# A retention layer with soft mixture of experts on one core: cleared tiles, a maximum kept as a column, eight PSUM banks for the last products, and inputs split into rows of 6 KB and 2 KB

## The chip, the cores and the metric

The kernel runs on one core of a Trainium2 chip. The metric is the device time of one execution in microseconds (us), as a median of several runs. The core's engines are called PE (TensorE, matrix products), DVE (VectorE), ACT (ScalarE), POOL (GpSimd) and SP (SyncE, which here issues all DMAs). All data is float32.

## What is computed

The inputs q, k and v have the shape (4 batches, 8 heads, 768 tokens, 64). A retention layer runs over the tokens, and its output, with the heads side by side (3072 tokens, 512 columns), goes through a soft mixture of 8 experts with 4 slots each:

```python
# retention, gamma[h] = 1 - 2**(-5-h)
for t in range(S):
    state = gamma * state + outer(k[:, :, t], v[:, :, t])
    y[:, :, t] = q[:, :, t] @ state / sqrt(D)
# soft mixture of experts, x = y as (3072, 512)
logits = x @ phi                                # (3072, 32 slots)
d = softmax(logits, over tokens)
slot_input = d.T @ x                            # (32, 512)
for e in range(8):                              # 4 slots of each expert
    slot_out[e] = relu(slot_input[e] @ w1[e]) @ w2[e]
c = softmax(logits, over slots)
out = c @ slot_out                              # (3072, 512)
```

## The kernel before, in words

**Steps and pairs.** The tokens are cut into chunks of 128, which makes 6 chunks x 4 batches = 24 steps; step i is chunk i//4 of batch i%4. The main loop (L448) runs over 12 pairs P of steps. For each step the scores of all heads are multiplied on PE (`score_mm`, L231) and masked on DVE (`score_mask`, L239); the carried state is applied (`carry_mm`, L255), the values are attended (`attend_mm`, L264), and the state of the batch is updated from keys by tokens and values (`state_mm`, L292, and `state_add`). POOL multiplies the decays into queries (`decay_q`, L216) and values (`decay_v`, L221) of the steps to come.

**Inputs.** `load_in` (L192) loads a step into one tile of 128 x 2048: columns 0 to 511 are the keys by head dimension (`kT`), 512 to 1023 the queries, 1024 to 1535 the values, 1536 to 2047 the keys by tokens (`kn`). Six such tiles are in turn (NIN). Step 0 has a load of its own. Ten steps (LEAN) load 1536 columns, 768 KB in rows of 6 KB (L203): those in TURNED, whose keys by tokens PE makes by transposing (`turn_k`, L210), and the last four, which need none. The other 13 (FULL) load the whole tile, 1 MB in rows of 8 KB (L205). The host lays the two kinds out in two arrays, `x3` and `x4` (L702).

**DMA order.** All loads and stores are issued by SP in the order of the program, on one queue. A load waits until its tile is free, and, since completion is counted on eight semaphores in turn, until the transfer eight places ahead of it has landed. Between the inputs, `load_weights` and `load_halves` issue the weights of the experts, 1 MB or twice 512 KB at a time, as many per pair as the table PACE says; later ones follow the products that set tiles free (L170). The eight outputs of 768 KB are issued at L648.

**Softmax over tokens.** Four steps make a group g (6 groups, the last is g = 5). `logits_mm` (L325) puts the logits of a group into the PSUM bank `sm`, and `logits` (L329) takes their maximum per slot and position, m, over all groups so far. For the last group it reduces the bank (L335) to the negated maximum `nmx`, then takes the minimum with the negated maximum of the groups before (L336) into column 1 of `nmc`. From this come the exponentials (L337) and the product `nj` (L541), which PE turns (L545) so that the four positions of each slot can be brought to one maximum.

**Experts.** After the last group, `hidden` (L584) multiplies the slots by w1, `hidden_t` turns the result and writes it, with the relu (L602), into two tiles `hT`, which hold zeros elsewhere; POOL clears them at L612, 128 x 1024 each. Then three blocks of output columns (256, 128 and 128 wide) are summed over experts in PSUM (L659, banks A0 and A1 in turn). `finish` (L623) repeats each block's slots with `rep` (L631, bank Y0) and multiplies them with the combine weights `cT` (L642): 4 products to each half of a 128-wide part, each in a bank of its own, taken in turn from the five in `co_tags` (L619). ACT and DVE copy the products out in turn (L647), and the half is stored (L648). The parts of block 0 and 1 are woven between the sums of the next block; the last block's come after everything.

Of the kernel before, what the change touches and what calls it, by code (L numbers as in the profile page):

```python
# [9 lines left out]
F32 = mybir.dt.float32  # L10
F32R = mybir.dt.float32r
AF = mybir.ActivationFunctionType
ALU = mybir.AluOpType
# [4 lines left out]
C = 128  # L18
# [5 lines left out]
NSLOT = 32  # L24
# [20 lines left out]
PACE = (1, 1, 1, 2, 1, 2, 1, 2, 2, 0, 2, 2)  # L45
TURNED = (0, 1, 2, 3, 4, 8, 12)
SIW = 48
LEAN = [i for i in range(1, NSTEP) if i in TURNED or i >= NSTEP - B]
FULL = [i for i in range(1, NSTEP) if i not in LEAN]

K_MASK, K_VSC, K_YT = 0, 128, 176
K_ID, K_QT, K_GC, K_J, K_ALL = 272, 400, 496, 500, 504
# [32 lines left out]
def retention_soft_moe_kernel(  # L85
    ctx: ExitStack,
    tc: tile.TileContext,
    in3: bass.AP,
    in4: bass.AP,
    phi: bass.AP,  # L90
    w1: bass.AP,
    w2: bass.AP,
# [99 lines left out]
    def load_in(i):  # L192
        t = large(inp)
        st[i] = dict(kT=t[:, 0:512].rearrange("p (g t) -> p g t", t=C),
                     qT=t[:, 512:1024].rearrange("p (g t) -> p g t", t=C),
                     v=t[:, 1024:1536].rearrange("p (h e) -> p h e", e=D),
                     kn=t[:, 1536:2048].rearrange("p (h d) -> p h d", d=D))
        if i == 0:
            nc.sync.dma_start(t[:, 0:1024], first_[0])
            nc.sync.dma_start(first, first_[1])  # L200
            st[i]["v"] = first[:, K_ALL:K_ALL + 512].rearrange("p (h e) -> p h e", e=D)
        elif i in LEAN:
            nc.sync.dma_start(t[:, 0:1536], in3[LEAN.index(i)])  # L203
        else:
            nc.sync.dma_start(t, in4[FULL.index(i)])  # L205

    def turn_k(i, name, ident=ident):
        kp = bank(name)
# [107 lines left out]

    gs = {}

    def logits_mm(g, js):
        q = gs.setdefault(g, {})  # L320
        if "ltp" not in q:
            q["ltp"] = bank("sm", (128, C))
        for p in range(NPAIR):
            for j in js:
                nc.tensor.matmul(q["ltp"][32 * j:32 * j + 32, :], phis[:, p, :], st[GRP * g + j]["yT"][:, p, :],  # L325
                                 start=(p == 0), stop=(p == NPAIR - 1), skip_group_check=True,
                                 tile_position=(0, 32 * j))

    def logits(g):  # L329
        q = gs[g]  # L330
        lt = q["ltp"]
        q["pT"] = small("pT", [128, C])
        if g == NGRP - 1:
            nmx = small("nmx", [128, 1])
            nc.vector.tensor_reduce(nmx, lt, AX.X, ALU.max, negate=True)  # L335
            nc.vector.tensor_scalar(nmc[:, 1:2], nmx, nmc[:, 0:1], None, ALU.min)  # L336
            nc.scalar.activation(q["pT"], lt, AF.Exp, bias=nmc[:, 1:2], scale=1.0, accum_out=zc[:, 1:2])  # L337
            return
        nm = nmc[:, 0:1] if g == NGRP - 2 else small("nm", [128, 1])
        q["m"] = small("m", [128, 1], bufs=2)  # L340
        if g == 0:
            nc.vector.tensor_reduce(q["m"], lt, AX.X, ALU.max)
        else:
            mg = small("mg", [128, 1])
            nc.vector.tensor_reduce(mg, lt, AX.X, ALU.max)
            nc.vector.tensor_scalar(q["m"], mg, gs[g - 1]["m"], None, ALU.max)
        nc.vector.tensor_scalar(nm, q["m"], -1.0, None, ALU.mult)
        turn_l(g)
        q["z"] = zrun if g == 0 else small("z", [128, 1])
        nc.scalar.activation(q["pT"], lt, AF.Exp, bias=nm, scale=1.0, accum_out=q["z"])  # L350
        if g > 0:
            q["al"] = small("al", [128, 1])
            nc.scalar.activation(q["al"], gs[g - 1]["m"], AF.Exp, bias=nm, scale=1.0)
# [94 lines left out]
    for P in range(NPP):  # L448
        last = P == NPP - 1
        g = P // 2  # L450
        load_weights(PACE[P])
        if 2 * P + NIN < NSTEP:
            load_in(2 * P + NIN)
            load_in(2 * P + NIN + 1)
        else:
            weight_pool[0] = inp
        if not last:
            for i in (2 * P + 2, 2 * P + 3):
                decay_q(i)
            if P % 2 == 0 and 0 < P < NPP - 2:  # L460
                next_chunk()
            for i in (2 * P + 2, 2 * P + 3):
                decay_v(i)
            if P == 1:
                for a in range(4):
                    qd = slice(32 * a, 32 * a + 32)
                    nc.gpsimd.tensor_copy(rep[qd].rearrange("p (j s) -> p j s", s=NSLOT),
                                          ident[qd, 32 * a:32 * a + 32].unsqueeze(1).broadcast_to([32, GRP, NSLOT]))
        if P == 0:
            score_mm(2)  # L470
            score_mask(2)
            attend_mm(0, (1,))
            attend_copy(0)
            state_mm(0)
            state_add(0)
            score_mm(3)
            score_mask(3)
            natural_mm(0, names=("A0", "A1"))
            natural_copy(0)
            turn_k(2, "sm")  # L480
            turn_k(3, "A0")
            decay_table(qtab, K_QT)
            continue
        carry_mm(P)
        if last:
            dispatch_u(g - 1, ["A0"])
            logits_mm(g, (0, 1))
            load_halves(2)
            load_weights(2)
        attend_mm(P)  # L490
        if last:
            load_halves(1, sall)
            break
        attend_copy(P)
        if P < NPP - B // 2:
            state_mm(P)
            state_add(P)
        if 2 * P + 2 in TURNED:
            turn_k(2 * P + 2, "A0")
        natural_mm(P)  # L500
        natural_copy(P)
        if P % 2 == 0 and P > 0:
            turn_mm(g - 1)
            turn_copy(g - 1)
        if P % 2 == 1:
            if g > 0:
                dispatch_u(g - 1, ["S"])
            logits_mm(g, range(GRP))
            if g > 0:
                dispatch_acc(g - 1)  # L510
                combine_b(g - 1)
            if g > 1:
                dispatch_z(g - 1)
        score_mm(2 * P + 2)
        score_mask(2 * P + 2)
        score_mm(2 * P + 3)
        score_mask(2 * P + 3)
        if P % 2 == 1:
            logits(g)
            if g > 0:  # L520
                combine_c(g - 1)
        if P % 2 == 0 and P > 0:
            combine_a(g - 1)
# [80 lines left out]
    for hf in range(2):  # L604
        for g2 in range(2):
            for k in range(NK):
                hidden(hf, g2, k)
                load_weights(1)
                if (hf, g2, k) == (0, 0, 0):
                    hT = [slot().rearrange("p (f e s) -> p f e s", e=NE, s=NSLOT) for _ in range(2)]  # L610
                    for t in hT:
                        nc.gpsimd.memset(t, 0.0)  # L612
                    combine_b(NGRP - 1)
                    combine_c(NGRP - 1)
                if (hf, g2, k) == (1, 0, 0):
                    hidden_t(0)
    load_weights(len(weights))

    co_tags = ["sm", "A2", "Y1", "A3", "S"]  # L619
    pend = []  # L620
    n_co = [0]

    def finish(cb, op):  # L623
# [11 lines left out]
        for m in range(w // 128):  # L635
            for h in range(2):
                ot = large(big)[:, 0:12 * C].rearrange("p (c j t) -> p c j t", j=B, t=C)
                cps = []
                for j in range(B):
                    cp = bank(co_tags[n_co[0] % len(co_tags)]).rearrange("p (c t) -> p c t", t=C)[:, 0:3]  # L640
                    n_co[0] += 1
                    nc.tensor.matmul(cp, s4[32 * j:32 * j + 32, m * 128:(m + 1) * 128],  # L642
                                     cT[32 * j:32 * j + 32, 3 * h:3 * h + 3, :], start=True, stop=True,
                                     skip_group_check=True, tile_position=(32 * j, 0))
                    cps.append(cp)
                for j in range(B):
                    (nc.scalar.copy if j % 2 else nc.vector.tensor_copy)(ot[:, :, j, :], cps[j])  # L647
                nc.sync.dma_start(out[c0 + m * 128:c0 + (m + 1) * 128, h * 12 * C:(h + 1) * 12 * C],  # L648
                                  ot.rearrange("p c j t -> p (c j t)"))
                for _ in range(BURST[cb]):  # L650
                    yield

    for cb, (c0, w) in enumerate(BLOCKS):
        op = bank(("A0", "A1")[cb % 2])
        units = ([(g, 4 * hf + f) for hf in range(2) for g in range(2) for f in range(4)] if cb == 0 else
                 [(g, fc) for g in range(2) for fc in range(NFC)])
# [19 lines left out]
def lay_out(q, k, v, moe_phi, moe_w1, moe_w2):  # L676
# [16 lines left out]
    for cb, (c0, w) in enumerate(BLOCKS):  # L693
# [3 lines left out]
        else:  # L697
            x = x.reshape(NE // 2, 2, NFC, 128, w).transpose(0, 3, 1, 2, 4)
        w2.append(x.reshape(-1, 128, 2 * FF))
    kt, qt, vn = tr(k), tr(q), nat(v)  # L700
    x = np.concatenate([kt, qt, vn, nat(k)], axis=2)
    return dict(x3=x[LEAN][:, :, 0:1536], x4=x[FULL], phi=phi,  # L702
                w1=w1, w2=np.concatenate(w2),
                first=np.stack([np.concatenate([kt[0], qt[0]], axis=1),
                                np.concatenate([constants(), vn[0], np.zeros((128, 1024 - K_ALL - 512), f)], axis=1)]))
# [21 lines left out]
```

## Time and profile before

| what | value |
|---|---|
| median of 3 runs | 158.97 us (158.67 to 159.25) |
| profiled execution, its own time | 159.04 us |
| span of the profile | 157.3 us |
| mean granted TensorE clock | 0.977 |
| busy: PE, DVE, ACT, POOL | 146.4, 78.3, 39.5, 59.7 us |
| moved by DMA | 62.81 MB, mean 399 GB/s |

The profile's times count from the start of its span; 159.04 - 157.3 = 1.7 us of the execution's time lie around the span. Idle time of an engine is put down to what ended it. The busy time of PE counts matmuls with modelled ends, so a busy PE is not PE at its peak. A DMA's issue on SP takes a fraction of a microsecond and isn't its transfer; the profile tells how long after the issue the transfer landed. The DMA share is the mean busy share of the core's 16 DMA engines.

### The profile page before, as it was taken

The page shows a single profiled execution, that of the slowest core. Times are in us where ns is not written, and L with a number is a line of the kernel's source. Part 1 is how long each engine was busy: PE and PEld are TensorE (multiplying, and loading weights), DVE is VectorE, ACT ScalarE, POOL GpSimd, SP SyncE. Part 2 cuts the span into 40 slices and gives each one's busy share as a digit, 9 for nine tenths or more (in the row PEclk, how much of TensorE's full clock was granted, in tenths as well). Part 3 has the DMA queues.
Part 4 walks back from the last instruction along what each step waited for, and adds up shares of the span by engine and source line. Part 5 has one row for each costly group of instructions (what it writes and reads, how often), then busy time and mean ns, then how long its engine had stood idle before and what let it go on. Part 6 is the DMA issues. An engine that isn't in the chain of part 4 may idle for free.

```text
span 157.3 us, 5480 instructions
## 1 busy us (share of the span) xinstructions
PE 146.4 (93%) x2410; PEld 107.6 (68%) x2410; DVE 78.3 (50%) x189; ACT 39.5 (25%) x95; POOL 59.7 (38%) x66
## 2 busy tenths in 40 slices
PE   8989999999999999999998989979999999999760
PEld 2569999997998699979996867755233455566520
DVE  0359517572956485758573855567210102564240
ACT  3312442315142306130514033231000000444030
POOL 0352796784837386474838275050100000000000
PEclk9999999999999999999999999999999999999955
DMA  5999999999999999999999999999999999999974
GB/s 172 400 402 429 423 413 420 417 423 415 413 416 417 421 417 421 415 417 417 409 421 415 417 406 413 405 382 424 401 421 425 423 419 421 415 413 401 388 298 192
DMA packets 9960, 62.81 MB, mean 399 GB/s; under 512 B 1104, under 2 KB 1232, under 8 KB 4560
## 3 DMA queue, kind: packets, MB, share of 16 engines
q1 hardware_dynamic: 9936, 62.46, 96.9%
q8 instruction: 19, 0.31, 0.8%
q14 instruction: 5, 0.04, 0.1%
HBM read 56.16 MB, written 6.29 MB: 397 GB/s over the span
## 4 chain that ended last, share of the span: by engine, by line
PE 86%; DMA 5%; DVE 2%; issue 1%; SPq 1%; ACT 0%
PE A L231 14%; PE Y L264 14%; PE A L659 9%; PE A L308 7%; PE Y L255 6%; PE S L292 6%; DMA b<-in_x_dram 5%; PE Y L584 4%; PE A L584 4%; PE sm L325 4%; PE S L383 3%; PE A L642 2%; PE S L642 2%; PE A L210 1%; PE sm L642 1%
## 5 line engine op out<-in xcount | busy, mean ns | idle before, releaser
L239 DVE TENSOR_TENSOR r<-A,kt 128x512 f32<-128x512 f32 x46 | 28.7, 684 | 18.5 <-PE A L231 18.5
L216 POOL TENSOR_TENSOR b<-b,qtab 128x512 f32<-128x512 f32 x20 | 25.4, 1275 | 22.4 <-DMA b<-in_x_dram 19.0
L231 PE MATMUL A<-b 64*128 64x128 f32 x384 | 25.2, 279 | 0.8 <-DMA b<-in_x_dram 0.6
L231 PEld LDWEIGHTS A<-b 64*128 64x128 f32 x384 | 22.6, 187 | 3.7 <-issue 1.8
L221 POOL TENSOR_TENSOR b<-b,kt 128x512 f32<-128x512 f32 x23 | 23.6, 1043 | 3.4 <-DMA b<-in_x_dram 3.4
L264 PE MATMUL Y<-r,b 128*64 128x128 f32 x352 | 22.4, 276 | 0.4 <-issue 0.4
L264 PEld LDWEIGHTS Y<-r,b 128*64 128x64 f32 x352 | 19.1, 137 | 2.8 <-issue 2.2
L659 PE MATMUL A<-b,r 128*32 128x128 f32 (+1 forms) x336 | 15.9, 300 | 0.0
L315 ACT COPY r<-A 128x512 f32<-128x512 f32 x23 | 12.4, 591 | 10.0 <-PE A L308 10.0
L659 PEld LDWEIGHTS A<-b,r 128*32 128x32 f32 x336 | 10.3, 110 | 6.4 <-issue 4.4
L308 PE MATMUL A<-kt,r 128*128 128x128 f32 x96 | 13.4, 279 | 0.3 <-ACT r L283 0.3
L292 PE MATMUL S<-b 128*64 128x64 f32 x304 | 11.2, 222 | 1.1 <-issue 1.1
L308 PEld LDWEIGHTS A<-kt,r 128*128 128x128 f32 x96 | 10.4, 140 | 1.7 <-ACT r L283 0.5
L292 PEld LDWEIGHTS S<-b 128*64 128x64 f32 x304 | 10.6, 138 | 1.3 <-issue 1.3
L255 PE MATMUL Y<-b,sst 64*64 64x128 f32 x304 | 10.6, 276 | 0.0
L415 POOL TENSOR_TENSOR cn<-cn,cz 128x128 f32<-128x128 f32 x6 | 2.4, 399 | 20.0 <-DVE cz L414 7.1
L284 DVE COPY r<-Y 128x512 f32<-128x512 f32 x9 | 6.2, 692 | 6.2 <-PE Y L264 6.2
L255 PEld LDWEIGHTS Y<-b,sst 64*64 64x64 f32 x304 | 8.2, 132 | 1.2
L642 PE MATMUL A<-cT,r 32*128 32x384 f32 x26 | 9.0, 559 | 0.0
L325 PEld LDWEIGHTS sm<-r,phis 128*32 128x32 f32 x192 | 6.2, 110 | 3.3 <-issue 3.3
L301 DVE TENSOR_TENSOR sst<-sst,S 128x256 f32<-128x256 f32 x16 | 6.0, 418 | 3.3 <-PE S L292 3.3
L325 PE MATMUL sm<-r,phis 128*32 128x128 f32 x192 | 7.4, 273 | 0.0
(140 smaller groups left out, 179.0 us busy)
## 6 DMA issues: line engine op xcount, KB each, us to landing
b<-in_w_dram SPq DMA_DIRECT2D x29, 1024.0 KB, 14.5
b<-in_x_dram SPq DMA_DIRECT2D x13, 1024.0 KB, 12.2
b<-in_x_dram SPq DMA_DIRECT2D x10, 768.0 KB, 11.4
out_dram<-b SPq DMA_DIRECT2D x8, 768.0 KB, 7.5
r<-in_w_dram SPq DMA_DIRECT2D x5, 512.0 KB, 11.2
b<-in_first_dram SPq DMA_DIRECT2D x1, 512.0 KB, 3.7
r<-in_first_dram SPq DMA_DIRECT2D x1, 512.0 KB, 4.5
sst<-in_w_dram SPq DMA_DIRECT2D x1, 512.0 KB, 11.9
```

The source lines that it names most:

```text
L216: nc.gpsimd.tensor_tensor(q, q, qtab, ALU.mult)
L221: nc.gpsimd.tensor_tensor(v, v, vsc[:, i // B, a:b].unsqueeze(2).broadcast_to([128, b - a, D]), ALU.mult)
L231: nc.tensor.matmul(s["sc"][r][:, g, :], s["kT"][half(r), g, :], s["qT"][half(r), g, :], start=True, stop=True, skip_group_check=True)
L239: nc.vector.tensor_tensor(s["A"][:, r, g:g + n], s["sc"][r][:, g:g + n], mask.unsqueeze(1).broadcast_to([128, n, C]), ALU.mult)
L255: nc.tensor.matmul(p["y"][k][b][half(half_of(r, g)), gl, :], sst[(2 * P + k) % B][half(r), g, :], s["qT"][half(r), g, :], start=(gl == 0 a ...
L264: nc.tensor.matmul(pr[P]["y"][k][g // 2][half(half_of(r, g)), g % 2, :], s["v"][:, 2 * g + r, :], s["A"][:, r, g, :], start=(P < B // 2 an ...
L292: nc.tensor.matmul(S_[half(r), k, g, :], s["kn"][:, 2 * g + r, :], s["v"][:, 2 * g + r, :], start=True, stop=True, skip_group_check=True)
L308: nc.tensor.transpose(X[k][:, g * 128:(g + 1) * 128], pr[P]["yT"][:, k, g, :], ident)
L325: nc.tensor.matmul(q["ltp"][32 * j:32 * j + 32, :], phis[:, p, :], st[GRP * g + j]["yT"][:, p, :], start=(p == 0), stop=(p == NPAIR - 1), ...
L584: nc.tensor.matmul(hp[hf][32 * j:32 * j + 32, :], si0[:, a:a + NSLOT], w1t[hf, g, k][:, j * 512:(j + 1) * 512], start=(g == 0 and k == 0), ...
L642: nc.tensor.matmul(cp, s4[32 * j:32 * j + 32, m * 128:(m + 1) * 128], cT[32 * j:32 * j + 32, 3 * h:3 * h + 3, :], start=True, stop=True, s ...
L659: nc.tensor.matmul(op[32 * j:32 * j + 32, :w], hT[fc // 4][:, fc % 4, 4 * g + j, :], w2t[4 * g + j, cb, fc], start=(n == 0), stop=(n == le ...
```

## The change

Four things are edited.

1. Every step but step 0 now loads its 1536 columns in rows of 6 KB from `x3`; the 13 steps in FULL load their keys by tokens in a second DMA, 256 KB in rows of 2 KB, from a new array `kn`. The set of 13 steps is the same.
2. The tiles `hT` are cleared by ACT, which copies a constant zero, instead of by POOL. The place in the program stays.
3. The bank of the last group's logits gets one more column. In pair 10, `logits_bank` copies the maximum m of the groups before into it; the last reduction then runs over 129 columns and gives the negated maximum over all groups at once, and the minimum (L336) goes.
4. The last block's products take eight banks in turn (`last_tags`) instead of five; the blocks before keep the five.

```diff
-LEAN = [i for i in range(1, NSTEP) if i in TURNED or i >= NSTEP - B]
-FULL = [i for i in range(1, NSTEP) if i not in LEAN]
+FULL = [i for i in range(1, NSTEP - B) if i not in TURNED]
...
-        elif i in LEAN:
-            nc.sync.dma_start(t[:, 0:1536], in3[LEAN.index(i)])
         else:
-            nc.sync.dma_start(t, in4[FULL.index(i)])
+            nc.sync.dma_start(t[:, 0:1536], in3[i - 1])
+            if i in FULL:
+                nc.sync.dma_start(t[:, 1536:2048], kn_[FULL.index(i)])
...
+    def logits_bank(g):
+        q = gs.setdefault(g, {})
+        q["ltm"] = bank("sm", (128, C + 1))
+        q["ltp"] = q["ltm"][:, 0:C]
+        if g == NGRP - 1:
+            nc.vector.tensor_copy(q["ltm"][:, C:C + 1], gs[g - 1]["m"])
+
     def logits_mm(g, js):
         q = gs.setdefault(g, {})
         if "ltp" not in q:
-            q["ltp"] = bank("sm", (128, C))
+            logits_bank(g)
...
         if g == NGRP - 1:
-            nmx = small("nmx", [128, 1])
-            nc.vector.tensor_reduce(nmx, lt, AX.X, ALU.max, negate=True)
-            nc.vector.tensor_scalar(nmc[:, 1:2], nmx, nmc[:, 0:1], None, ALU.min)
+            nc.vector.tensor_reduce(nmc[:, 1:2], q["ltm"], AX.X, ALU.max, negate=True)
...
+        if P == NPP - 2:
+            logits_bank(NGRP - 1)
         score_mm(2 * P + 2)
...
-                    hT = [slot().rearrange("p (f e s) -> p f e s", e=NE, s=NSLOT) for _ in range(2)]
+                    hT = [slot() for _ in range(2)]
                     for t in hT:
-                        nc.gpsimd.memset(t, 0.0)
+                        nc.scalar.copy(t, nc.const_aps.tensor(0.0, [128, 1024], F32))
+                    hT = [t.rearrange("p (f e s) -> p f e s", e=NE, s=NSLOT) for t in hT]
...
+    last_tags = ["S", "sm", "A2", "Y1", "A3", "A1", "A0", "Y0"]
...
-                    cp = bank(co_tags[n_co[0] % len(co_tags)]).rearrange("p (c t) -> p c t", t=C)[:, 0:3]
+                    tags = co_tags if cb < len(BLOCKS) - 1 else last_tags
+                    cp = bank(tags[n_co[0] % len(tags)]).rearrange("p (c t) -> p c t", t=C)[:, 0:3]
...
     for cb, (c0, w) in enumerate(BLOCKS):
+        if cb == len(BLOCKS) - 1:
+            n_co[0] = 0
...
-    x = np.concatenate([kt, qt, vn, nat(k)], axis=2)
-    return dict(x3=x[LEAN][:, :, 0:1536], x4=x[FULL], phi=phi,
+    return dict(x3=np.concatenate([kt, qt, vn], axis=2)[1:], kn=nat(k)[FULL], phi=phi,
```

On SP, the start of the queue after the first loads read like this before (`b<-in_x_dram` is a step's input, `b<-in_w_dram` a tile of weights; steps 5 to 9):

```order
L205 DMA b<-in_x_dram 128x2048
L167 DMA b<-in_w_dram 128x2048
L205 DMA b<-in_x_dram 128x2048 x2
L167 DMA b<-in_w_dram 128x2048
L203 DMA b<-in_x_dram 128x1536
L205 DMA b<-in_x_dram 128x2048
```

and it reads like this now:

```order
L204 DMA b<-in_kn_dram 128x512
L166 DMA b<-in_w_dram 128x2048
L202 DMA b<-in_x_dram 128x1536
L204 DMA b<-in_kn_dram 128x512
L202 DMA b<-in_x_dram 128x1536
L204 DMA b<-in_kn_dram 128x512
L166 DMA b<-in_w_dram 128x2048
L202 DMA b<-in_x_dram 128x1536 x2
L204 DMA b<-in_kn_dram 128x512
```

Each load of a whole tile has become two, the keys by tokens right behind the rest; the weights keep their places between the steps.

On DVE, the last group's softmax (from the reduction of the bank `sm` on) was this:

```order
L335 TENSOR_REDUCE nmx<-sm 128x1
L336 TENSOR_SCALAR nmc<-nmx,nmc 128x1
L541 TENSOR_SCALAR nj<-kt,nmc 128x4
L315 COPY r<-A_1628 128x512
L375 COPY pl<-Y_1646 128x128
```

and is this now, with the rows around the copied maximum of pair 10 ahead of it:

```order
L283 COPY r<-Y_1460 128x2x256
L323 COPY sm<-m 128x1
L238 TENSOR_TENSOR r<-A_1515,kt 128x512
...
L340 TENSOR_REDUCE nmc<-sm 128x1
L547 TENSOR_SCALAR nj<-kt,nmc 128x4
L314 COPY r<-A_1642 128x512
L379 COPY pl<-Y_1658 128x128
```

The minimum between the reduction and `nj` is gone, and one copy of a column stands ahead of the masks of steps 22 and 23.

On PE, the last block's eight products, behind the repeat of its slots (`Y` is bank Y0 in the first row), were these (names begin with the bank's letter; the number tells banks of a letter apart):

```order
L631 MATMUL Y_2105<-os,rep 128x128
L642 MATMUL S<-cT,r 128x384
L642 MATMUL sm<-cT,r 128x384
L642 MATMUL A_2113<-cT,r 128x384
L642 MATMUL Y_2115<-cT,r 128x384
L642 MATMUL A_2123<-cT,r 128x384
L642 MATMUL S<-cT,r 128x384
L642 MATMUL sm<-cT,r 128x384
L642 MATMUL A_2129<-cT,r 128x384
```

and are these now:

```order
L639 MATMUL Y_2117<-os,rep 128x128
L651 MATMUL S<-cT,r 128x384
L651 MATMUL sm<-cT,r 128x384
L651 MATMUL A_2125<-cT,r 128x384
L651 MATMUL Y_2127<-cT,r 128x384
L651 MATMUL A_2135<-cT,r 128x384
L651 MATMUL A_2137<-cT,r 128x384
L651 MATMUL A_2139<-cT,r 128x384
L651 MATMUL Y_2141<-cT,r 128x384
```

The banks S and sm (and A2, the fourth of the second half) no longer come twice: the second four products go to A3, A1, A0 and Y0.

More of the change, by code (lines that the diff above doesn't have):

```diff
@@ L88, in retention_soft_moe_kernel @@
     in3: bass.AP,
-    in4: bass.AP,
+    kn_: bass.AP,
     phi: bass.AP,
```

## The prediction

> **What bounds the kernel now.** I read the page first, and in it the chain of work that ended last and the DMA queue, because the two disagree.
>
> ```profile
> q1 hardware_dynamic: 9936, 62.46, 96.9%
> ...
> PE 86%; DMA 5%; DVE 2%; issue 1%; SPq 1%; ACT 0%
> ```
>
> By the chain TensorE (PE) is the bound. By the queue, the one DMA queue that carries all inputs, weights and outputs keeps the 16 DMA engines occupied for 96.9% of the span. So I asked for the busy times by stretches of time; the last two columns are the DMA share (mean over the 16 engines) and GB/s.
>
> ```profile
> 110.00:130.00 20.00, 20.00 (x242) 7.91 (x234) 2.51 (x10) 0.96 (x3) 0.40 (x1) 1.00 1.01 417
> 130.00:144.00 14.00, 13.89 (x263) 8.40 (x258) 6.50 (x14) 4.30 (x10) 0.00 (x0) 1.00 1.01 417
> ...
> 148.00:151.00 3.00, 2.80 (x16) 1.50 (x16) 1.53 (x4) 0.86 (x2) 0.00 (x0) 0.86 0.61 249
> ```
>
> The DMA engines are full (1.01) up to 144 us at least. In 148 to 151 us the mean share falls to 0.61, although output transfers are under way: some engines have run dry and others have not. Which of them sets the end is told by the last three outputs: when they are issued (tail timeline below: 150.19 for the second) and when they land.
>
> ```profile
> L648 SPq DMA_DIRECT2D out_dram<-b x3: 332/332/333, 145.7 to 152.4; - x3
> ...
> DMA to landing us min/median/max: 3.9/4.3/6.9
> ```
>
> Issued at 145.7, 150.2 and 152.4, they need 6.9, 4.3 and 3.9 us and land at 152.6, 154.5 and 156.3. The issues are 4.5 and 2.2 us apart, the landings 1.9 and 1.8 us. An output of 768 KB (786,432 bytes) at the 417 GB/s of the rows above takes 1.89 us: the landings follow each other at the queue's own pace, whatever the issues do. So I read the end like this: a transfer is spread over the DMA engines and lands when its last engine is done; the engine furthest behind has had work without a break up to 156.3 us, and the span ends 1.0 us later, at 157.3. To the end, the queue's total work counts; PE's chain runs beside it. The last output is close to the border, though, because 3.9 us is about what a 512 KB transfer needs from an empty queue (3.7 us, the first row of the next fence).
>
> ```profile
> b<-in_first_dram SPq DMA_DIRECT2D x1, 512.0 KB, 3.7
> ...
> phis<-in_phi_dram SPq DMA_DIRECT2D x1, 64.0 KB, 9.2
> ```
>
> The Trainium skill, page "Perfetto Trace Analysis", section "What "DMA-bound" means", names specific DMA engines as one such bound and advises large descriptors there; by that, splitting 8 KB rows is the wrong direction, as in my sum.
>
> **Part 1, the split inputs.** Thirteen steps loaded one tile of 1 MB in rows of 8 KB. Now each is loaded as 768 KB in rows of 6 KB and 256 KB in rows of 2 KB. The bytes stay the same; what comes new is 13 times one more transfer and 128 more rows. The ten other steps are loaded as before. The trace has no 2 KB rows. Two prices bound them. First, the rates in a stretch with rows of 8 KB (weights), one with mostly rows of 6 KB (outputs) and one with many rows of 4 KB (half tiles of weights), in this order:
>
> ```profile
> 122.00:128.00 6.00, 6.00 (x92) 3.04 (x88) 0.78 (x3) 0.37 (x1) 0.00 (x0) 1.00 1.01 422
> 139.50:143.00 3.50, 3.50 (x73) 2.16 (x76) 1.58 (x5) 0.88 (x3) 0.00 (x0) 1.00 1.01 421
> 99.50:107.00 7.50, 6.62 (x89) 4.68 (x85) 4.30 (x16) 2.27 (x7) 2.18 (x3) 1.00 1.02 397
> ```
>
> 422 against 421 GB/s says that rows may cost nothing: lower bound 0. With 4 KB rows the rate is 397, 6% less. Rows of 2 KB have twice as many per byte, so I take twice the loss, 12%, as the upper bound: 256 KB take 0.62 us at 422 GB/s, 12% is 0.075 us, times 13 is 1.0 us. Second, the nearest thing to "one more transfer and 128 more rows" is the small load of phi, 128 rows in 64 KB. The issues stand in SyncE's timeline, and the landing of the input ahead of it is the longer of the pair below.
>
> ```profile
> 3.29 0.44 SPq L432 DMA_DIRECT2D phis<-in_phi_dram  x1
> L203 SPq DMA_DIRECT2D b<-in_x_dram x2: 432/550/668, 2.1 to 2.6; - x2
> ...
> DMA to landing us min/median/max: 8.2/9.0/9.7
> ```
>
> The input lands at 2.6 + 9.7 = 12.3 us, phi at 3.3 + 9.2 = 12.5 us. Of these 0.2 us the 64 KB take 0.155 us at 422 GB/s; the rest, 0.045 us, is what a transfer and its rows cost beyond bytes. Times 13 that is 0.6 us, inside the bounds, and I take it: **+0.6 us of queue work, range 0 to 1.0**. The Trainium skill, page "DMA: Bandwidth & Descriptors", section "Why small descriptors are slow", gives a fixed overhead of about 3 cycles per packet; with the 850 MHz of its specifications and the 8 rows that an engine takes of 128, this is an estimate of 13 x 8 x 3.5 ns = 0.4 us. The trace's 0.6 goes into the sum, and no run yet shows 2 KB rows. Its "Bandwidth" section fits 2 us plus bytes to a transfer; paid 13 times in series that would be 26 us, and phi, landing 0.2 us behind its neighbour, speaks against it in a full queue.
>
> SyncE gets 13 more issues of about 0.4 us (0.44 in phi's row), 6 us in all; it makes 1% of the chain. Scores and the decay of queries wait only for the 6 KB part, which lands some 0.6 us earlier, and the state products wait for the keys, which land when the tile did. PE hardly waits there (DMA is 5% of the chain), so I count nothing for it.
>
> **Part 2, cleared tiles and the maximum.** The timeline around the last group's softmax:
>
> ```profile
> 103.27 1.84 POOL L612 MEMSET r<- 128x1024 f32 x2
> 103.33 0.29 DVE L335 TENSOR_REDUCE nmx<-sm 128x1 f32<-128x128 f32 x1 [0.55 <-PE sm L325]
> 103.66 0.21 DVE L336 TENSOR_SCALAR nmc<-nmx,nmc 128x1 f32<-128x1 f32 x1
> 103.80 0.60 PE L423 MATMUL A<-const-float32-0.0 128*1 128x128 f32 x4
> 103.91 1.23 DVE L541 TENSOR_SCALAR nj<-kt,nmc 128x4 f32<-128x4 f32 x1
> ...
> 105.28 0.36 PE L545 MATMUL S<-nj,rep 128*128 128x4 f32 x2 [0.88 <-DVE r L315]
> ```
>
> Three facts: the clearing on GpSimd runs from 103.27 to 105.11; the tiny product nj ends with it, at 105.14; and PE waits 0.88 us for that.
>
> ```profile
> L413 DVE TENSOR_SCALAR cz<-cz 128x4 f32<-128x4 f32 x6 | 1.0, 170 | 0.2
> ...
> L428 ACT COPY kt<-r 128x504 f32<-128x504 f32 x1 | 0.6, 615 | 3.7 <-DMA r<-in_first_dram 3.7
> ```
>
> The same shape takes 0.17 us elsewhere. Without the clearing nj is ready 1.06 us sooner, and 0.25 us more goes with L336 (103.66 to 103.91). Of these 1.3 us PE can use 0.9: its warming products end at 104.40, and it starts at 105.28 now. On ScalarE the clearing costs 2 copies of 128x1024, each about twice the 0.615 us of 128x504: 2.5 us. They stand behind L407 and ahead of L590, where ScalarE is idle for 5.9 us:
>
> ```profile
> 116.15 0.37 ACT L590 COPY r<-A 128x256 f32<-128x256 f32 x1 [5.93 <-PE A L584]
> ```
>
> So they are hidden; without that cover they would delay the copies of the hidden layer by 2.5 us. The new copy of the maximum into the logits bank stands on VectorE ahead of the masks of steps 22 and 23 and has to wait for ScalarE to read the bank's last content:
>
> ```profile
> 95.26 0.28 ACT L368 COPY pl<-sm 128x128 f32<-128x128 f32 x1
> ...
> 95.94 0.69 DVE L239 TENSOR_TENSOR r<-A,kt 128x512 f32<-128x512 f32 x1 [2.16 <-PE A L231]
> ```
>
> It can start at 95.54 and the mask starts at 95.94 anyway: a copy of one column, shorter than the 0.21 us of L336, is hidden. Sum of part 2: **PE 0.9 us earlier from 105 us on**.
>
> **Part 3, eight banks.** The tail's timeline:
>
> ```profile
> 149.58 1.01 DVE L647 COPY b<-A 128x384 f32<-128x384 f32 x2
> ...
> 150.19 2.51 SPq L648 DMA_DIRECT2D out_dram<-b  x2
> 151.03 0.56 DVE L647 COPY b<-sm 128x384 f32<-128x384 f32 x1 [0.44 <-PE sm L642]
> 151.03 0.48 ACT L647 COPY b<-S 128x384 f32<-128x384 f32 x1 [1.02 <-issue]
> 151.86 0.48 ACT L647 COPY b<-A 128x384 f32<-128x384 f32 x1 [0.35 <-PE A L642]
> ```
>
> Today the second four products wait for banks that the first four hold, and the last copy ends at 152.34. With a bank each, VectorE copies four in a row, two in 1.01 us: the second of them ends at 150.59, the fourth at 151.1 (ScalarE's are shorter). The last output is issued 1.2 us sooner. With part 2, the last two outputs are issued 0.9 and 2.1 us sooner, at 149.3 and 150.3.
>
> **The sum.** What is late next is the queue. The output ahead of those two lands at 152.6 now, being queued for 6.9 us; an earlier issue does not land it earlier. The next two follow 1.9 us apart, at 154.5 and 156.3, and part 1 adds 0.6 to all. So 0 of the 2.1 us arrive, and 0.6 us come on top: from the profiled execution's 159.04 us (span 157.3 and 1.7 around it) to **159.6 us**. The median before, 158.97, is 0.1 below that execution; against it this is +0.6 us, 0.4%. A measurement of this kernel can tell about 0.3%, 0.5 us, from no change.
>
> **The rivals.**
> *A, PE's gain arrives at the tail.* If my reading of the last landings is wrong and each output lands a fixed time after its issue, the naive sum is 159.04 - 2.1 = 156.9. But the last two would then be issued 1.0 us apart (149.3 and 150.3), and 768 KB take 1.9 us. So the last lands 1.9 us after the one before, which lands 0.9 sooner: the end moves by 0.9, to 158.1. For it: 3.9 us for the last output is close to the 3.7 us of an empty queue, and a share of 0.61 shows that most engines have slack. Against it: three landings at the queue's pace. It decides if the engines furthest behind are not the same ones all along. Chance 0.2.
> *B, the rows cost nothing* (421 against 422 GB/s): the end stays with the queue, 159.0, no change. Chance 0.2.
> *C, the queue runs dry.* A transfer waits for the one eight places ahead of it (the issues' waits go over eight semaphores in turn); with 256 KB transfers among them, the eight in flight hold less, and SyncE may issue an input too late. Each dry spell would cost the start of a transfer, 3.7 us less the 1.3 us that 512 KB take, 2.4 us: with one of them 159.6 + 2.4 = 162.0. It decides when seven transfers hold less than some 4 us of work. Against it: keys alternate with inputs and weights, so at least four of the seven bring 768 KB or more, over 7 us at 1.9 us each. Chance 0.07.
> *My forecast*, 159.0 to 160.1 with 159.6 in the middle: chance 0.53.
>
> **How the numbers follow.** Faster by over 0.3%: A but for 0.01 of it, 0.19. Within 0.3% (158.5 to 159.45): that 0.01, B, and the part of my forecast where the split costs under 0.4 us or so, 0.01 + 0.2 + 0.13 = 0.34. Slower: the rest of my forecast and C, 0.4 + 0.07 = 0.47. The range goes from A's 158.1, with 0.1 for its copies' spread, to 160.1, the upper bound of part 1: 158.0 to 160.1. It leaves out C and the tails of A, under 0.2. The forecast's own range is 159.0 to 160.1.
>
> **What would show it.** Right: nj takes about 0.2 us and PE's wait ahead of L545's product is gone; the hidden layer starts 0.9 us sooner; the two last outputs are issued about 1 us apart, yet land 1.8 to 1.9 us apart, with over 5 us from issue to landing for the last; the share of the DMA engines stays at 1.0 up to the tail. Wrong: the last output lands within 4 us of an issue near 150.3 (A), or the DMA share falls under 1 before 140 us (C), or the mask of step 22 starts later because of the copied maximum.

## The result and the profile after

The kernel after takes 160.19 us (median of 5 runs, 160.13 to 160.24), the kernel before 158.99 us in the same session (158.67 to 159.25). The ratio is 1.0068, with a 95% interval of 1.0043 to 1.0093: 1.2 us slower. That is 0.6 us above the forecast of 159.6, and 0.09 us above the upper end of the range, 160.1. In what follows, medians are over all runs of a kernel, while ratios leave out disturbed runs (for one, those over 1.5% above the fastest of their kernel), so the two can differ a little. The profiled execution took 160.24 us, its span 158.5.

First the page of the kernel after, its DMA queue and its chain of waits:

```profile
span 158.5 us, 5493 instructions
...
q1 hardware_dynamic: 11808, 62.46, 97.1%
...
PE 91%; DVE 1%; issue 1%; ACT 1%; DVEq 0%; ACTq 0%
```

The bytes are the same 62.46 MB. The packets went from 9936 to 11808. The time they took is 97.1% of 158.5, 153.9 us for each DMA engine; before it was 96.9% of 157.3, 152.4 us. So the queue has 1.5 us more to do, and the span is 1.2 us longer. By the chain alone PE would look even more like the bound than before (91% for 86%), yet PE became faster, as the next views show.

The stretches of time of the kernel after, with the same columns as before (at the end the granted clock, the DMA share and GB/s):

```profile
110.00:130.00 20.00, 20.00 (x248) 8.30 (x244) 1.87 (x7) 1.79 (x4) 0.40 (x1) 1.00 1.01 417
...
130.00:144.00 14.00, 13.89 (x256) 8.24 (x252) 6.94 (x15) 4.71 (x12) 0.00 (x0) 1.00 1.01 414
...
148.00:151.00 3.00, 0.62 (x8) 0.01 (x1) 1.95 (x4) 1.63 (x4) 0.00 (x0) 1.00 0.91 375
```

Up to 144 us the engines are as full as before. In 148 to 151 us PE is busy for 0.62 us (before: 2.80), because it is done, and the DMA share is 0.91 (before: 0.61): the rest of the work now lies in the queue.

The last two outputs of the kernel after:

```profile
L657 SPq DMA_DIRECT2D out_dram<-b x2: 333/333/333, 149.1 to 150.0; - x2
...
DMA to landing us min/median/max: 6.5/7.0/7.5
```

They are issued at 149.1 and 150.0, which is 1.1 and 2.4 us sooner than before. They need 6.5 and 7.5 us (before: 4.3 and 3.9) and land at 155.6 and 157.5, 1.9 us apart and 1.1 to 1.2 us later than before.

The timeline around the last group's softmax, after:

```profile
103.22 0.29 DVE L340 TENSOR_REDUCE nmc<-sm 128x1 f32<-128x129 f32 x1 [0.55 <-PE sm L331]
...
103.54 0.23 DVE L547 TENSOR_SCALAR nj<-kt,nmc 128x4 f32<-128x4 f32 x1
...
103.69 0.60 PE L427 MATMUL A<-const-float32-0.0 128*1 128x128 f32 x4
...
104.22 0.38 PE L551 MATMUL S<-nj,rep 128*128 128x4 f32 x2
```

The clearing has left GpSimd, nj takes 0.23 us (before: 1.23), the minimum of L336 is gone, and the product on nj starts at 104.22 (before: 105.28), with no wait for VectorE. Of these 1.06 us, 0.11 were there ahead of it: the reduction itself starts at 103.22, for 103.33 before. The gain reaches the hidden layer, whose first products are shown here for the kernel before and then for the kernel after:

```profile
108.95 1.06 PE L584 MATMUL A<-b,qtab 128*32 128x512 f32 x8
```

```profile
107.91 7.07 PE L590 MATMUL A<-b,qtab 128*32 128x512 f32 x64
```

PE is 1.04 us earlier from there on. The covers of part 2 and the tail of part 3, in the timeline of the kernel after:

```profile
95.15 0.28 ACT L372 COPY pl<-sm 128x128 f32<-128x128 f32 x1
95.46 0.16 DVE L323 COPY sm<-m 128x1 f32<-128x1 f32 x1 [1.80 <-ACT pl L372]
95.82 1.89 DVE L238 TENSOR_TENSOR r<-A,kt 128x512 f32<-128x512 f32 x3 [0.20 <-PE A L230]
...
109.08 1.97 ACT L618 COPY r<-const-float32-0.0 128x1024 f32<-128x1024 f32 x2
115.05 0.37 ACT L596 COPY r<-A 128x256 f32<-128x256 f32 x1 [4.00 <-PE A L590]
...
148.47 1.48 DVE L656 COPY b<-A 128x384 f32<-128x384 f32 x3
...
149.16 0.51 ACT L656 COPY b<-Y 128x384 f32<-128x384 f32 x1
```

The copied maximum ends at 95.62, and the masks start at 95.82, released by PE. The two clearing copies take 1.97 us, and ScalarE is still idle for 4.0 us behind them. At the tail VectorE copies three tiles in a row without a wait, up to 149.95. Everything that the change does on the engines gains what it should, and nothing of it reaches the end.

### The profile page after: what moved, and what is told of

The parts are those of the page before. It is cut to its first block, busy times and chain, and to the rows that moved or that the text cites. A ratio compares the mean times of both kernels' runs of the same rounds, so it can differ in the third digit from the quotient of the medians.

```text
span 158.5 us, 5493 instructions
## 1 busy us (share of the span) xinstructions
PE 145.6 (92%) x2410; PEld 107.4 (68%) x2410; DVE 78.6 (50%) x189; ACT 41.1 (26%) x97; POOL 58.1 (37%) x64
## 3 DMA queue, kind: packets, MB, share of 16 engines
q1 hardware_dynamic: 11808, 62.46, 97.1%
## 4 chain that ended last, share of the span: by engine, by line
PE 91%; DVE 1%; issue 1%; ACT 1%; DVEq 0%; ACTq 0%
PE A L230 16%; PE Y L263 14%; PE A L670 9%; PE A L307 8%; PE Y L254 6%; PE S L291 6%; PE Y L590 4%; PE A L590 4%; PE sm L331 4%; PE sm L427 3%; PE S L387 3%; PE sm L651 1%; PE A L209 1%; PE S L651 1%; PE Y L651 1%; PE Y L639 1%
## 5 line engine op out<-in xcount | busy, mean ns | idle before, releaser
L411 ACT ACTIVATE cn<-cn 128x128 f32<-128x128 f32 x6 | 1.9, 310 | 22.1 <-DVE cn L410 22.1
```

## Experiments

All were timed in five rounds beside the kernel before, whose median was 158.9 to 159.0 in each session. Where time went missing, the theories were: the split's rows, the split's transfers, the edits of parts 2 and 3, or something beside the edits.

**Parts 2 and 3 alone: the kernel after with the inputs of before.**

```diff
+        elif i in LEAN:
+            nc.sync.dma_start(t[:, 0:1536], in3[LEAN.index(i)])
         else:
-            nc.sync.dma_start(t[:, 0:1536], in3[i - 1])
-            if i in FULL:
-                nc.sync.dma_start(t[:, 1536:2048], kn_[FULL.index(i)])
+            nc.sync.dma_start(t, in4[FULL.index(i)])
...
```

> The changed kernel with its inputs as before (one transfer of 1 MB, 8 KB rows), so the cleared tiles, the copied maximum and the eight banks alone. Queue theory (the DMA queue's work sets the end, the split alone costs): as before, 158.7 to 159.3 us, with the last output issued near 150.0 but landing near 156.2. Rival 1 (PE's gain arrives and the split costs more than it shows): about 158.1 us. Rival 2 (one of the three compute edits is what costs): 159.8 us or more.

Measured: 159.31 us, ratio 1.0032 (1.0015 to 1.0050). Its last two outputs:

```profile
L658 SPq DMA_DIRECT2D out_dram<-b x2: 332/332/332, 149.2 to 150.1; - x2
...
DMA to landing us min/median/max: 5.4/5.8/6.3
```

They are issued 1.0 and 2.3 us sooner than before and land at 154.6 and 156.4, 0.1 behind before's (154.5 and 156.3). Rival A, that PE's gain arrives, is out: with the queue's work as before, issues 1.0 and 2.3 us sooner gain nothing. But the kernel isn't equal to before either: it is 0.3% slower, and no part of the forecast accounts for that.

**The split alone: the kernel before with the split inputs** (the same lines the other way round).

> The kernel before with the split inputs alone. Queue theory: as the changed kernel, 160.0 to 160.4 us, since the compute edits neither gain nor cost. Rival 1 (PE's gain of some 0.9 us arrives in the changed kernel): about 161.1 us. Rival 2 (the compute edits cost): near 159.0 us.

Measured: 159.84 us, ratio 1.0052 (1.0035 to 1.0070), so 0.8 us for the split (0.6 to 1.1). In the trace:

```profile
L647 SPq DMA_DIRECT2D out_dram<-b x2: 332/332/333, 150.1 to 151.5; - x2
...
DMA to landing us min/median/max: 4.9/5.1/5.3
```

By the finer times of the trace the last output lands at 156.85, 0.6 later than before's 156.24. Rival B, that the rows cost nothing, is out. The 160.0 to 160.4 us that were expected for the split alone are missed, though: part of what the change costs lies elsewhere, as e1 says too.

**Rows without transfers: each of the 13 tiles as one transfer of 256 rows of 4 KB.**

```diff
-            nc.sync.dma_start(t, in4[FULL.index(i)])
+            nc.sync.dma_start(t.rearrange("p (a f) -> p a f", a=2), in4[FULL.index(i)].rearrange("a p f -> p a f"))
...
```

> The kernel before, its 13 full tiles each loaded by one transfer of 256 rows of 4 KB in place of 128 rows of 8 KB: 128 more rows per tile, as many as the split brings, and no more transfers. If the split's cost lies in the number of rows: 159.8 to 160.2 us. If it lies in the number of transfers: near 159.0 us.

Measured: 159.77 us, ratio 1.0052 (1.0032 to 1.0072). One transfer with 128 more rows costs the same as two transfers with 128 more rows, to within the intervals' 0.3 us. So the rows pay, and the additional transfer costs nothing that can be seen here. The packets (each row is one) say the same: by their medians in the trace, a 6 KB and a 2 KB packet of the split take 236 + 84 = 320 ns, two of 4 KB 2 x 161 = 322 ns, one of 8 KB 312 ns. With 13 x 8 = 104 more rows for each DMA engine, 8 to 10 ns each make 0.8 to 1.0 us. The trace of the kernel before already holds this price, and the forecast could have read it there: by their medians, packets of 512 bytes take 27 ns, of 4 KB 159 and of 6 KB 234, so each 2 KB take 75 ns and the packet itself about 9. 104 times 9 ns is 0.94 us.

**Transfers without rows: each of the 13 tiles as two transfers of 64 partitions, rows of 8 KB.**

```diff
-            nc.sync.dma_start(t, in4[FULL.index(i)])
+            for r in (slice(0, 64), slice(64, 128)):
+                nc.sync.dma_start(t[r], in4[FULL.index(i), r])
```

> The kernel before, its 13 full tiles each loaded by two transfers of 64 partitions, rows still 8 KB: 13 more transfers, no more rows. If the split's cost lies in the number of transfers: near 160.2 us. If it lies in the number of rows: 159.0 to 159.3 us.

Measured: 202.13 us, ratio 1.2585 (1.2526 to 1.2644). Neither theory had that. The profiled execution took 206.75 us, the quickest of the six 198.75. The stretch from 20 to 40 us, first of the kernel before, then of this one:

```profile
20.00:40.00 20.00, 20.00 (x393) 17.66 (x395) 10.71 (x24) 6.64 (x16) 14.38 (x18) 1.00 1.01 418
```

```profile
20.00:40.00 20.00, 12.25 (x206) 10.66 (x206) 5.88 (x12) 3.99 (x10) 8.21 (x11) 0.88 1.02 248
```

The DMA share still reads full (1.02), at 248 GB/s in place of 418: a stretch in which loads to 64 partitions alternate with weights to 128 runs at little over half the rate while all engines read busy. Once these loads are through (the last lands at 124.7 us), the rate is back: 413 GB/s from 130 to 190 us. The run tells nothing about the number of transfers, which the one before settles; why it is so slow wasn't pursued.

**The unexplained 0.3%: where the tiles lie.** In the traces, e1's transfers land 0.2 to 0.4 us behind before's between 77 and 91 us, where no edited instruction has run yet (the first is the copied maximum at 95 us). That is a hint and no more: earlier in the same traces they run from 0.2 us ahead to 0.2 us behind. What had changed that early was one thing only. With the minimum went its tile nmx, 32 bytes in each partition, and all large tiles behind it (the pools inp, ring and big, where nearly all transfers land or start) moved down by 32 bytes: from 64 bytes past a multiple of 256 to 32 past one. (These places are added up from the sizes of the tiles ahead; the traces hold no addresses.) The kernel before with that shift alone:

```diff
-    nmc = small("nmc", [128, 2])
+    nmc = small("nmc", [128, 3])
...
-            nmx = small("nmx", [128, 1])
+            nmx = nmc[:, 2:3]
```

> The kernel before with one thing changed: the small tile nmx becomes a third column of the tile nmc. No instruction, transfer or order changes; the one effect is that all large tiles behind it in SBUF start 32 bytes lower, as they do in the kernel after and in the unsplit one (e1), so that they start at an odd multiple of 32 bytes in place of a multiple of 64. Theory S (the 0.3 to 0.4 us that e1 lost without any split come from the shifted addresses, as its landings lag from the start and its 8 KB packets read 313 ns for 312): 159.3, ratio 1.002 to 1.003, last weight and outputs land 0.2 to 0.4 us later than before. Theory I (they come from the edited instructions, or from how instruction fetches fall on the DMA engines): 158.9, ratio 1.000, landings as before.

Measured: 159.57 us, ratio 1.0030 (1.0011 to 1.0048). No instruction or transfer differs from before. The last two outputs:

```profile
L648 SPq DMA_DIRECT2D out_dram<-b x2: 332/332/332, 150.4 to 151.9; - x2
...
DMA to landing us min/median/max: 4.5/4.7/4.9
```

By the finer times of the trace the last lands at 156.72, 0.5 later than before. An 8 KB packet takes 313 ns by the median, for 312 before; with the 5376 such packets spread over 16 engines, 1 ns is 0.34 us. So the shift costs 0.5 us by the times (0.2 to 0.8). The counterpart is e1 with the 32 bytes kept:

```diff
+            small("nmx", [128, 1])
             nc.vector.tensor_reduce(nmc[:, 1:2], q["ltm"], AX.X, ALU.max, negate=True)
```

> The unsplit kernel e1 (parts 2 and 3 of the change alone) with the dropped 32-byte tile kept, unused, so that every large tile stands where it stood before. Theory S (shifted addresses cost e1 its 0.3 to 0.4 us): 158.9, ratio 1.000, last output lands at 156.2, although the last two outputs are issued at about 149.2 and 150.1. Theory I (edited instructions or fetches): 159.3, ratio 1.003, the last output at 156.4 or later.

Measured: 159.04 us, ratio 0.9997 (0.9971 to 1.0024): the 0.3% is gone by the median, though the interval is wide enough to hold some of it. The trace does not show it gone. Its execution took 159.25 us, and its last two outputs are issued 0.9 us later than expected and land where theory I had them, the last at 156.4:

```profile
L659 SPq DMA_DIRECT2D out_dram<-b x2: 332/332/332, 150.1 to 151.0; - x2
...
DMA to landing us min/median/max: 4.5/5.0/5.4
```

What tells the two theories apart in the traces is the packets. In each of the four unsplit kernels 19 to 32 of the 8 KB packets take over 15% more than the median; the mean of the others is 313.0 and 313.3 ns where the tiles stand at the old place (before and e6) and 314.4 ns in both kernels with the shift (e1 and e5). 1.1 to 1.4 ns make 0.4 to 0.5 us, the cost that e5 measured. (The mean over all packets hides it: 315.8 and 316.0 against 316.0 and 316.2.) The same line put into the kernel after:

> The kernel after with the dropped 32-byte tile kept, unused, so that the large tiles start at a multiple of 64 bytes as before. If the costs of the split (0.8 by e2) and of the shift (0.3 to 0.5 by e1 and e5) add up: 159.7 to 159.9, ratio 1.004 to 1.006, 0.3 to 0.5 under the kernel after. Rival (rows of 6 and 2 KB cost the same wherever they land, and the two don't add up): 160.2, ratio 1.0075.

Measured: 159.61 us, ratio 1.0043 (1.0022 to 1.0064). That is just under the 159.7 to 159.9 expected, and by the median 0.6 us under the kernel after; by the two ratios, each beside the kernel before of its own session, it is 0.4 us with some 0.5 either way. The profiled execution took 160.18 us, as long as the kernel after. So this run agrees with the sum of two costs but would not show it alone; its 8 KB packets are back at a median of 312 ns, for 313 in the kernel after.

If 32 bytes the one way cost, other addresses may gain. The kernel before with an unused tile of 192 bytes ahead, so that the large tiles start at multiples of 512:

```diff
+    small("pad", [128, 48])
     sall = small("sst", [128, B * NPAIR * D])
```

> The kernel before with an unused tile of 192 bytes ahead of the large tiles, so that they start at a multiple of 512 bytes (before: a multiple of 64 that is an odd one; e5: an odd multiple of 32). Nothing else changes. Theory N (only the step of 64 bytes counts): 159.0, ratio 1.000, 8 KB packets 312 ns as before. Theory L (each larger power of two helps a little more): 158.7 or less, ratio 0.998 or less, 8 KB packets 311 ns or less.

Measured: 157.41 us, ratio 0.9898 (0.9871 to 0.9925). This is 1.5 us faster than the kernel before and 2.8 faster than the kernel after, the fastest here of those that leave nothing out. Theory N is out. Theory L has the sign right, with far more than its figure; whether each power of two adds its part wasn't tried. Its page and last outputs:

```profile
span 155.5 us, 5480 instructions
...
q1 hardware_dynamic: 9936, 62.46, 96.6%
```

```profile
L649 SPq DMA_DIRECT2D out_dram<-b x2: 332/332/332, 149.1 to 151.3; - x2
...
DMA to landing us min/median/max: 3.2/3.2/3.3
```

The same 9936 packets take 96.6% of 155.5, 150.2 us for each engine, 2.2 less than before. An 8 KB packet takes 309 ns by the median for 312, and 311.1 by the mean for 315.8, which is 1.6 of the 2.2 us. Now the last two outputs land 3.2 to 3.3 us after their issue: the queue no longer sets the end, PE's chain does, and so of 2.2 us some 1.5 arrive. Even these need PE's part: the two are issued 1.0 us sooner than before, and with before's issues the last would have landed no earlier than 152.4 + 3.2 = 155.6, for 156.3.

**Does PE's gain exist at all?** Two kernels with 13 x 256 KB less to load: the keys by tokens are left out, and the keys by channels are read in their place, so the state products are of other numbers.

```diff
+        if i in FULL:
+            st[i]["kn"] = t[:, 0:512].rearrange("p (h d) -> p h d", d=D)
...
-        elif i in LEAN:
-            nc.sync.dma_start(t[:, 0:1536], in3[LEAN.index(i)])
         else:
-            nc.sync.dma_start(t, in4[FULL.index(i)])
+            nc.sync.dma_start(t[:, 0:1536], in3[i - 1])
```

From the kernel before:

> The kernel before with 3.25 MB less to load: the keys by tokens of 13 steps are not loaded (the keys by channels are read in their place, so the state products are of other numbers; all instructions of PE, VectorE and ScalarE stay). That takes 13 x 256 KB, at 422 GB/s 8 us, off the DMA queue. Forecast's reading (before, the queue's work sets the end, with PE close behind: last output issued at 152.4): now PE's chain sets it, the last output lands 3.7 to 3.9 us after an issue near 152.2, so 158.6 to 158.9, ratio 0.997 to 1.000. Rival (the queue alone sets the end and PE has much slack): down by more than 2 us, ratio under 0.985.

Measured: 157.64 us, ratio 0.9917 (0.9888 to 0.9946), between the two theories. From the unsplit kernel:

> The unsplit kernel with the old addresses (e6: PE's part of the change alone), with the same 13 loads of keys by tokens left out as in e7 (other numbers in the state products). Forecast's reading (PE's gain exists and only the queue hides it): it arrives once the queue is short. The last two outputs are issued at about 149.2 and 150.1, the first of them lands some 4 us later and the last 1.9 us behind it, at 155.1 to 155.3, so 157.8 to 158.0, 0.9 to 1.1 us under e7, ratio 0.992 to 0.994. Rival (PE's earlier end is worth nothing in any case, since the outputs' own transfers set the end): equal to e7 within 0.3 us.

Measured: 156.99 us, ratio 0.9872 (0.9846 to 0.9899), 0.65 us under e7 (0.9 to 1.1 were expected), with some 0.6 either way when the two intervals are combined. The last two outputs, of e7 and then of e8:

```profile
L647 SPq DMA_DIRECT2D out_dram<-b x2: 332/332/333, 149.7 to 151.1; - x2
...
DMA to landing us min/median/max: 3.3/3.5/3.7
```

```profile
L658 SPq DMA_DIRECT2D out_dram<-b x2: 332/332/333, 148.8 to 149.7; - x2
...
DMA to landing us min/median/max: 3.3/3.8/4.2
```

With a short queue the first of the two outputs lands 3.3 us after its issue in both, and the last follows at 154.8 in e7 and 153.9 in e8: of the 0.9 and 1.4 us by which e8 issues the two sooner, 0.9 arrive, since two outputs issued 0.9 us apart still land 1.9 apart. It is rival A's arithmetic, in a kernel where A's condition holds. What the expectations had wrong is e7: PE's own chain got shorter. Its chain of waits:

```profile
PE 92%; DVE 2%; issue 1%; ACT 1%
```

The 5% of DMA in the chain of before are gone, and the last outputs are issued 0.5 and 1.3 us sooner. PE did wait 0.6 us for an input in the trace of before, which fits the first of these; that the missing loads are the reason is argued, not shown, as the chain of the kernel after has no DMA in it either, with all its loads.

**Trading queue for PE: more steps turned on TensorE.** From e6, two and four more steps whose keys by tokens are not loaded but made on PE:

```diff
-TURNED = (0, 1, 2, 3, 4, 8, 12)
+TURNED = (0, 1, 2, 3, 4, 6, 8, 12, 16)              # e10
+TURNED = (0, 1, 2, 3, 4, 6, 8, 10, 12, 14, 16)      # e12
```

> The unsplit kernel with the old addresses (e6) and two more steps (6 and 16) whose keys by tokens are not loaded but turned on TensorE out of the keys by channels; the output stays the reference's. It takes 2 x 256 KB, 1.24 us at 422 GB/s, off the queue and adds 2 x 0.57 us to PE (four products by the identity each). Forecast's reading (the queue's work sets the end of e6, PE's chain ends about 1 us ahead of it): the queue's end falls by 1.2 to 157.8, PE's end is e8's 157.0 plus 1.1, 158.1; the later counts: 157.9 to 158.3, ratio 0.993 to 0.996, faster than before. Rival (PE's chain is what sets the end): slower by up to 1.1, 159.5 to 160.1.

> As e10, with four more steps turned (6, 10, 14, 16). Queue 2.5 us less than in e6, PE 2.3 us more. Forecast's reading (the later of the two ends counts): PE's end is e8's 157.0 plus 2.3, 159.3, and the queue's 156.5, so 159.0 to 159.5, ratio 1.000 to 1.003, slower than e10. Rival (the queue alone sets the end): 156.6, faster than e10.

Measured: 159.68 us for two more, ratio 1.0028 (1.0003 to 1.0054); 158.71 us for four more, ratio 0.9939 (0.9905 to 0.9973), which rests on the six lower of its twelve runs, while the median of all is only 0.2 us under before's 158.91. Both expectations failed, and so did their order. The first number lies in the range of its rival, that PE's chain sets the end (159.5 to 160.1), but then four more would have to be slower still. The profiled execution of the first took 157.81 us, as expected, but the other eleven runs took 159.15 to 160.30; the kernel with four more had one run of 156.48 among runs of 158.2 to 159.4. Only the profiled execution has a trace, so what the longer runs do differently stays open. These two say nothing safe about the trade.

## Why the prediction was right in its course and short in its size

- *The queue sets the end, not PE's chain.* Right. PE's issues came 1.1 and 2.4 us sooner and the landings came later, at their own 1.9 us; e1, and e6 with the old addresses (159.04 us), show the same without any split. With a short queue the gain arrives in the landings (e8's are 0.9 us sooner than e7's); by the times it is 0.65 us, some 0.6 either way. The forecast saw the last output close to the border because an empty queue had taken 3.7 us for 512 KB; outputs of 768 KB take 3.2 to 3.3 us in e7, e8 and e9 when nothing is ahead, so the 3.9 us of before stood some 0.6 us inside. That one DMA engine is behind all others up to the end, as the forecast read the share of 0.61, no view here shows.
- *Part 1, +0.6 us, range 0 to 1.0.* Right in cause and sign; e2 gives 0.8 (0.6 to 1.1). The forecast had priced "a transfer and its rows" as one from phi's landing; e4 shows that the rows carry it, 8 to 10 ns each. That the forecast's 0.045 us came so near is in part luck, for it is what is left of two landings read to 0.1 us; from the finer 12.29 and 12.48 the same sum gives 0.5. The Trainium skill, page "DMA: Bandwidth & Descriptors", section "Why small descriptors are slow", has about 3 cycles per packet, the 0.4 us of the prediction: that each packet costs something agrees with these runs, the size is half of what they show or less. The fit of 2 us plus bytes, which the prediction also names from the Trainium skill, stands in that page's section "Anatomy of one DMA — SWDGE (gpsimd) path", for transfers that GpSimd issues, and not in the section on bandwidth; paid in series it would have made 26 us, and e2's thirteen transfers cost 0.8 us with their rows.
- *Part 2, PE 0.9 us earlier; the clearing and the copied maximum hidden.* Right: 1.06 us at the product on nj, 0.95 of them without the reduction's earlier start, and 1.04 at the hidden layer; the clearing took 1.97 us, not 2.5, with 4.0 us of idle behind it.
- *Part 3, the outputs issued at 149.3 and 150.3.* Right: 149.1 and 150.0, for 150.2 and 152.4 before. That nothing of it arrives was right too.
- *The sum.* Here a term is missing. "0.25 us more goes with L336" was counted as an instruction; that its 32-byte tile goes too, and moves every large tile, was not looked at. By e5 that costs 0.5 us (0.2 to 0.8). With the split's 0.8 it makes 1.3, for 1.2 measured. Without the shift, e11 takes 159.61, just what the forecast gave; that it meets it so well is luck, with the split forecast at 0.6 and measured at 0.8. That e1's loss is the shift and nothing else rests on e6's median and on the packets' times; e6's interval leaves up to 0.2% for something else.
- *Why the address counts.* That stays open. By the medians, the 8 KB packets take 309 ns to multiples of 512 bytes, 312 to 64 bytes past a multiple of 256, 313 to 32 past one; loads of 6 KB take 234, 236 and 238. The Trainium skill, page "DMA: Bandwidth & Descriptors", section "How a descriptor splits into AXI transactions", says that a transaction starts at a 256-byte boundary, and that the bytes from there to an unaligned start are fetched for nothing, in beats of 32 bytes. That aligned rows are faster agrees with e9; by that rule 64 bytes past would cost a beat more than 32 past, and the runs have it the other way round. That account also speaks of what is fetched, and these loads write to the shifted places.
- *Rival C, the queue runs dry.* Out: from 10 to 100 us, where the split inputs are loaded, the share of the kernel after is 1.02 throughout.

## What to carry to other kernels

When the last transfers land at their own pace whatever their issues do, a faster engine is worth nothing until the queue has slack; look there first, and count rows, not transfers: the packets in the trace tell what a row costs. An edit that drops or adds even a 32-byte tile moves every tile behind it, so compare the addresses of the large DMA targets before and after, and try them at a multiple of 512 bytes: here one line of padding was worth 1.5 us, while nothing of the 2.4 us that the change gained on the engines arrived.

## What the runs showed that I had not expected

- Where DMA targets start in SBUF: +0.3% from 32 bytes lower, -1.0% from 192 bytes higher, with every instruction the same. Which power of two is needed (128, 256 or 512) wasn't tried, nor the padding together with parts 2 and 3, where e8 would let one expect PE's gain on top.
- With loads to 64 partitions in it, a stretch ran at 248 GB/s that ran at 418 with all to 128, with a DMA share of 1.02: the share shows that engines have work, not that bytes move.
- One profiled execution can stand 1.9 us beside the median of its kernel (157.81 and 159.68 in e10), more than the effect under study.
